# Block-sorted attention and a squared-ReLU FFN: the values of batches 1 to 3 sorted as rows in four array tiles, and turned by way of DRAM

## The chip, the cores and the metric

The kernel runs on one core of a Trainium2 chip. The metric is the device time of one execution in microseconds (us), and the median over several runs is compared. The engines are named as the profile names them: PE is TensorE (PEld its weight loads), DVE is VectorE, ACT is ScalarE, POOL is GpSimd and SP is SyncE. Here SP only issues DMAs. All DMA queues share 16 DMA engines.

## The reference

Four batches, eight heads, 768 tokens in eight blocks of 96, 64 values per head. A small 8 x 8 matrix per head is turned into a soft permutation P by five rounds of exponential and row and column normalisation. Keys and values are mixed over blocks with P. Each query block attends to its sorted block. The result, as 3072 rows of 512, goes through a two-layer network.

```python
P = sort_net
for _ in range(5):
    P = P - np.max(P, axis=-1, keepdims=True)
    P = np.exp(P)
    P = P / (np.sum(P, axis=-1, keepdims=True) + 1e-09)
    P = P / (np.sum(P, axis=-2, keepdims=True) + 1e-09)
...
k_sorted = np.einsum('bhij,bhjcd->bhicd', P, k_b).reshape(B, H, S, D)
v_sorted = np.einsum('bhij,bhjcd->bhicd', P, v_b).reshape(B, H, S, D)
...
scores = scale * np.matmul(q_b, k_sb.transpose(0, 1, 2, 4, 3))
scores = scores - np.max(scores, axis=-1, keepdims=True)
attn = np.exp(scores)
attn = attn / (np.sum(attn, axis=-1, keepdims=True) + 1e-09)
return np.matmul(attn, v_sb).reshape(B, H, S, D).astype(np.float32)
...
h = x @ w_in
r = np.maximum(h, 0.0)
g = s * (r * r) + b
return (g @ w_out).astype(np.float32)
```

## The kernel before, in words

**Layout.** A batch is cut into two halves of 384 tokens (TG), so the network has eight token groups t = 2b + half. ffn1(t) makes the squared hidden layer of one group (L395): eight pairs of 128-wide columns, each pair 8 matmuls on PE (L408), a relu on ACT (L422) and a multiply on DVE (L423). ffn2(t) multiplies it with w_out (L427): three output tiles of 128 tokens with 16 matmuls each (L433), then DVE scales and adds a bias (L454) and SP stores the tile (L457).

**Attention of one batch.** Raw keys, values and queries come by POOL's DMA queue, which casts to bf16 on the way (load, L84; load_q, L94, in eight DMAs of short rows). k_piece (L247) sorts 16 of 48 key positions with 32 matmuls of 64 columns, whose moving operand is a block-diagonal form of P (PD, build_pd L231); v_piece (L298) does the same for 16 of 64 value columns. For v_piece the raw values must lie with the value column outside and the position inside, so they are first copied into VP (permute, L165), by ACT for batch 0 and by POOL for the others (v_sort, L504, eight copies per batch). The sorted values stand in VS (L107), key position on the partitions and 66 numbers per head and block: 64 values and two ones. The ones make the sum of the attention weights come out of the same matmul as the attention output. s_piece (L311) makes the scores of one head pair and half, and their exponential on ACT; p_piece (L338) multiplies them with VS and DVE normalises into x; t_dma (L386) transposes x by a DMA of SP into XT, the input of ffn1. q_dma (L291) transposes the queries in the same way, in two DMAs.

**Order.** Each engine runs its instructions in the order of the program. The order is written by hand: ffn1 and ffn2 take a dictionary of slots, and the pieces in a slot are issued after the named pair of columns (ffn1) or group of four matmuls (ffn2, slots 0 to 11). Batch 0 is sorted at the start. While ffn2(2b) and ffn2(2b + 1) run, the pieces of batch n = b + 1 are woven in (L572 to L581). In ffn2(2b): K in slot 2, three of the four V pieces in slot 5, the last V and the first scores in slot 9, the first P in slot 11. The loads of batch 1 follow the weights on POOL's queue (L514); those of batches 2 and 3 are issued in the first slot of ffn1 (gated_loads, L555).

**Buffers.** rawp has two buffers each for raw keys, values and queries, psa three two-bank PSUM buffers that all pieces and ffn1 share, VP, KS and VS two each (for even and odd batches).

Of the kernel before, what the change touches and what calls it, by code (L numbers as in the profile page):

```python
# [9 lines left out]
FP = mybir.dt.float32  # L10
# [12 lines left out]
def kernel(  # L23
# [26 lines left out]
    KR = GAP + C2  # L50
    NG = NHP * NB
    VW = D + 2
    CK = 16
    scale = float(D) ** -0.5


    raw = [t.rearrange("b h (j z c) d -> b (h j z) (c d)", j=NB, z=2) for t in (q, k, v)]

    const = ctx.enter_context(tc.tile_pool(name="const", bufs=1))
    rawp = ctx.enter_context(tc.tile_pool(name="rawp", bufs=2))  # L60
    trp = ctx.enter_context(tc.tile_pool(name="trp", bufs=2))
    atp = ctx.enter_context(tc.tile_pool(name="atp", bufs=6))
    xp = ctx.enter_context(tc.tile_pool(name="xp", bufs=2))
# [3 lines left out]
    osb = ctx.enter_context(tc.tile_pool(name="osb", bufs=3))  # L67
    psa = ctx.enter_context(tc.tile_pool(name="psa", bufs=3, space=bass.MemoryType.PSUM))
    psb = ctx.enter_context(tc.tile_pool(name="psb", bufs=2, space=bass.MemoryType.PSUM))
    ctx.enter_context(tc.manual_schedule())  # L70


# [11 lines left out]
    def load(t, b, parts=1):  # L84
# [3 lines left out]
        for c in range(0, C2, n):  # L88
            nc.gpsimd.dma_start(out=ti[:, c:c + n, :].rearrange("p c d -> p (c d)"),
                                in_=raw["qkv".index(t)][b][:, c * D:(c + n) * D])  # L90

    QTOK = {}

    def load_q(b, ns=range(NB)):  # L94
# [4 lines left out]
        for n in ns:  # L99
# [2 lines left out]
    zeros = const.tile([128, 512], BF)  # L102
    nc.vector.memset(zeros[:, 0:128], 0.0)  # L103
    nc.vector.memset(zeros[:, 128:512], 0.0)  # L104
    VP = [const.tile([128, D, GAP], BF, name=f"vp{i}") for i in range(2)]
    KS = [const.tile([128, NG, 2, GAP], BF, name=f"ks{i}") for i in range(2)]
    VS = [const.tile([KR, 2 * NG, VW], BF, name=f"vs{i}") for i in range(2)]  # L107
    nc.vector.memset(VP[0][:, :, C2:GAP], 0.0)
    nc.vector.memset(KS[0][:, :, :, C2:GAP], 0.0)
    nc.vector.memset(sne[:, NB, :], 1e-9)  # L110

# [3 lines left out]
    idv = ident.rearrange("p (a e j z) -> p a e j z", a=NHP, e=2, j=NB)  # L115
    emat = const.tile([BH, B, 128], FP)
    nc.gpsimd.memset(emat, 0.0)
    nc.gpsimd.affine_select(out=emat, in_=emat, pattern=[[-H, B], [-1, H], [0, 2 * NB]], base=0,
                            channel_multiplier=1, compare_op=ALU.not_equal, fill=1.0)
    load("k", 0, 3)  # L120
    load_q(0, range(HB))
# [24 lines left out]
            fs = slice(c * (NF // 4), (c + 1) * (NF // 4))  # L146
            nc.gpsimd.dma_start(out=wo[:, fs, :], in_=wov[:, fs, :])

    def fill_vs(i):
        nc.gpsimd.memset(VS[i][:, :, D:VW], 1.0)  # L150
        nc.gpsimd.memset(VS[i][32:GAP, :, D:VW], 0.0)
        nc.gpsimd.memset(VS[i][32:C2, :, D:VW], 1.0)

    fill_vs(0)
    Z = []

    def warm(n, w=512):
# [4 lines left out]
                             start=True, stop=True)  # L162


    def permute(eng, b, src, cs=slice(0, C2), ds=slice(0, D)):  # L165
        o = VP[b % 2][:, ds, cs]
        i = src[:, cs, ds].rearrange("p c d -> p d c")
        if eng is nc.scalar:
            eng.copy(out=o, in_=i)
        else:  # L170
            eng.tensor_copy(out=o, in_=i)  # L171


    rstat = const.tile([BH, NB], FP)
    rrec = const.tile([BH, NB], FP)
    jsel = const.tile([128, NB], FP)
    bm = const.tile([128, 2 * 2 * NHP], FP)
    idle = [
        lambda: nc.vector.tensor_reduce(
            out=jsel, in_=ident.rearrange("p (h j z) -> p j h z", h=H, j=NB), axis=AX.XY, op=ALU.add),  # L180
# [8 lines left out]
    for it in range(5):  # L189
        nc.scalar.activation(out=sn, in_=sn, func=AF.Exp)  # L190
        if it >= 1:
            permute(nc.scalar, 0, v0f, slice((it - 1) * CV, it * CV))
        if it in (1, 2):
            idle[it - 1]()
        nc.vector.tensor_reduce(out=rstat, in_=sn, axis=AX.X, op=ALU.add)
        nc.vector.reciprocal(out=rrec, in_=rstat)
        nc.vector.tensor_tensor(out=sn, in0=sn, in1=rrec.broadcast_to([BH, NB, NB]), op=ALU.mult)
        if it == 4:
            break
        nc.vector.tensor_reduce(out=rstat, in_=sne.rearrange("p i j -> p j i"),  # L200
                                axis=AX.X, op=ALU.add)
        nc.vector.reciprocal(out=rrec, in_=rstat)
        nc.vector.tensor_tensor(out=sn, in0=sn, in1=spread(rrec, [[0, NB], list(rrec.ap[1])]),
                                op=ALU.mult)
# [11 lines left out]
                             rhs=sn.rearrange("p i j -> p (i j)"), start=True, stop=True)  # L216
        return pe

    def take_p(b0, n, pe):

        bs = slice(b0, b0 + n)
        tmp = rtp.tile([128, n * NB, NB], FP, tag=f"tmp{n}", name="tmp")
        nc.vector.tensor_tensor(out=tmp, in0=pe.rearrange("p b i j -> p (b i) j"),
                                in1=spread(jsel, [[0, n * NB], list(jsel.ap[1])]), op=ALU.mult)
        nc.vector.tensor_reduce(out=PT[:, bs].rearrange("p b i -> p (b i)"), in_=tmp, axis=AX.X,
                                op=ALU.add)
        cs = rtp.tile([128, n], FP, tag=f"cs{n}", name="cs")
        nc.vector.tensor_reduce(out=cs, in_=PT[:, bs], axis=AX.X, op=ALU.add)
        nc.vector.reciprocal(out=RC[:, bs], in_=cs)

    def build_pd(b):  # L231
        pd = const.tile([128, 2, 2, NG], BF, name=f"pd{b}")
        nc.vector.scalar_tensor_tensor(
            out=pd.rearrange("p e z (a i) -> p (e z a) i", i=NB),
            in0=spread(bm, [list(bm.ap[1]), [0, NB]]), scalar=RC[:, b:b + 1],
            in1=spread(PT[:, b], [[0, 4 * NHP], list(PT.ap[2])]), op0=ALU.mult, op1=ALU.mult)
        PD[b] = pd

    def evac(eng, out, in_):
        if eng == "A":  # L240
# [50 lines left out]
    def q_dma(b):  # L291
        qt = q_tile(b)
        for n0 in (0, HB):
            nc.sync.dma_start_transpose(
                out=qt[:, n0:n0 + HB].rearrange("p n a t -> p (n a) t"),
                in_=QTOK[b][:, n0:n0 + HB].rearrange("p n h d -> p (n h d)"))

    def v_piece(b, d0, eng):  # L298
        ps = psa.tile([128, CK, 2 * NG], FP, tag="a", name="tv")
        for d in range(CK):  # L300
            for z in range(2):
                nc.tensor.matmul(out=ps[z * GAP:(z + 1) * GAP, d, :],  # L302
                                 lhsT=VP[b % 2][:, d0 + d, :], rhs=PD[b][:, :, z, :],
                                 start=True, stop=True)
        evac(eng, VS[b % 2][:, :, d0:d0 + CK], ps[0:KR].rearrange("p d g -> p g d"))

    AT = {}
    X = {}
# [32 lines left out]
    def p_piece(b, half, hp, later=False):  # L341
        g0 = hp * NB + half * HB
        atf = AT.pop((b, half, hp)).rearrange("p e t -> p (e t)")
        if hp == 0:
            X[b, half] = xp.tile([BLK, HB, d_model], BF, tag="x", name="x")
        x = X[b, half]
        pv = psa.tile([128, 2, 512], FP, tag="a", name="pv")
        for e in range(2):
            for n in range(HB):
                c0 = (e * HB + n) * BLK  # L350
                m = 128 if c0 + 128 <= 2 * TG else BLK
                nc.tensor.matmul(out=pv[0:m, e, n * VW:(n + 1) * VW],  # L352
                                 lhsT=atf[:, c0:c0 + m], rhs=VS[b % 2][:, e * NG + g0 + n, :],
                                 start=True, stop=True)

        def norm():
            pvv = pv[0:BLK, :, 0:HB * VW].rearrange("p e (n w) -> p e n w", w=VW)
            rec = rtp.tile([BLK, 2, HB], FP, tag="rec", name="rec")
            nc.vector.reciprocal(out=rec, in_=pvv[:, :, :, D])
            nc.vector.tensor_tensor(  # L360
                out=x[:, :, hp * 128:(hp + 1) * 128].rearrange("p n (e d) -> p e n d", e=2),
                in0=pvv[:, :, :, 0:D],
                in1=rec.unsqueeze(3).broadcast_to([BLK, 2, HB, D]), op=ALU.mult)

        if later:
            return norm
        norm()
# [89 lines left out]
        nc.sync.dma_start(out=out[r0:r0 + 128, ns], in_=ot[:, ns])  # L457


    take_p(0, 1, spread_p(0, 1))  # L460
    build_pd(0)

    nc.gpsimd.tensor_copy(out=ones[:, 0:1], in_=PD[0][:, 0, 0, 0:1])
# [31 lines left out]
    nc.gpsimd.memset(sel, 0.0)  # L495
    for r in range(0, 128, 32):
        nc.gpsimd.memset(sel[r:r + 1], 1.0)
    nc.gpsimd.memset(VP[1][:, :, C2:GAP], 0.0)
    nc.gpsimd.memset(KS[1][:, :, :, C2:GAP], 0.0)
    fill_vs(1)  # L500
    for t, src in ((s_bc, moe_s), (b_bc, moe_b)):
        nc.gpsimd.dma_start(out=t, in_=src.to_broadcast([128, 1]))

    def v_sort(b):  # L504
        for i in range(8):
            permute(nc.gpsimd, b, RAW["v", b], ds=slice(i * 8, (i + 1) * 8))

    def loads(b):
        load("k", b)
        load("v", b)  # L510
        load_q(b)
        v_sort(b)

    loads(1)  # L514

# [19 lines left out]
        nc.scalar.activation(out=bias, in_=bps, func=AF.Copy, scale=b_bc)  # L535

    def K(b, i, eng): return lambda: k_piece(b, i * CK, eng)
    def V(b, i, eng): return lambda: v_piece(b, i * CK, eng)
    def SC(b, h, i): return lambda: s_piece(b, h, i)
    def SB(b, h, i): return lambda: s_banks(b, h, i)  # L540
    def P(b, h, i): return lambda: p_piece(b, h, i)
# [3 lines left out]
    def QB(b, n0, eng): return lambda: q_blocks(b, n0, eng)  # L545
# [2 lines left out]
    ffn1(0, {-1: [TP(0, 0, 2, "AD")], ("pre", 1): [QB(0, HB, "D"), QB(0, HB + 2, "D")],  # L548
             2: [SB(0, 1, 0)], 3: [SB(0, 1, 1), P(0, 1, 0)], 4: [SB(0, 1, 2), P(0, 1, 1)],
             5: [SB(0, 1, 3), P(0, 1, 2)], 6: [TP(0, 1, 0, "D"), P(0, 1, 3)]}, ahead=3)  # L550
    ffn1(1, {-2: [TP(0, 1, 2, "D")], 1: [lambda: take_p(1, B - 1, PB), PDB(1)], 4: [PDB(2)],
             5: [PDB(3), sum_w], 7: [make_bias]}, ahead=3)
    gate = const.tile([128, 1], BF)

# [7 lines left out]
    for b in range(B):  # L562
# [4 lines left out]
        if n == B:  # L567
            ffn2(2 * b, {})
            ffn2(2 * b + 1, {})
            break  # L570
        q_dma(n)
        s0 = {  # L572
            2: [K(n, 0, "A"), K(n, 1, "D"), K(n, 2, "A")],
            5: [V(n, 0, "D"), V(n, 1, "A"), V(n, 2, "D")],
            9: [V(n, 3, "D"), SC(n, 0, 0), SC(n, 0, 1)],
            11: [P(n, 0, 0), SC(n, 0, 2), SC(n, 0, 3)]}
        ffn2(2 * b, s0)
        ffn2(2 * b + 1, {0: [P(n, 0, 1)], 1: [P(n, 0, 2)],
                         2: [P(n, 0, 3), TD(n, 0), SC(n, 1, 0), SC(n, 1, 1)],
                         4: [P(n, 1, 0)], 5: [P(n, 1, 1), SC(n, 1, 2), SC(n, 1, 3)],  # L580
                         7: [P(n, 1, 2)], 8: [P(n, 1, 3), TD(n, 1)]})  # L581


# [28 lines left out]
```

## Time and profile before

| | us |
|---|---|
| Median of three runs (lowest, highest) | 229.03 (228.82, 230.14) |
| The profiled execution | 228.41 |
| Its span in the profile | 226.6 |
| PE busy in the span | 218.9 (97%) |
| DVE, ACT, POOL busy | 124.5, 99.5, 68.2 |
| ffn1 matmuls (L408), busy | 85.7 |
| ffn2 matmuls (L433), busy | 85.7 |
| V sorting matmuls (L302), busy | 10.0 |
| POOL's copies of values (L171), busy | 19.0 |

The profile shows one execution. Busy time of an engine is the time in which at least one instruction of it runs. The chain that ended last goes back from the last instruction, at each step to what released it, or to the instruction before it on its engine; a piece of work in it has a start and a duration. A group of instructions has its mean duration in ns, and ahead of it the engine's idle time with what ended it. Matmuls overlap in the pipeline, so the mean of one is longer than the distance between two.

### The profile page before, as it was taken

To read this page: it belongs to the slowest core of one execution; us is meant where nothing else is said; L and a number is where in the kernel's file an instruction comes from. 1 tells how busy PE (TensorE), PEld (TensorE's weight loads), DVE (VectorE), ACT (ScalarE), POOL (GpSimd) and SP (SyncE) were. 2 spreads that over 40 slices of the span, in tenths; PEclk is the share of its full clock that TensorE was granted. 3 is DMA by queue.
4 is the path that set the end of the run, shared out by engine and by line. 5 is a ranking of instruction groups with operands and counts; after the bars stand their busy time and mean duration, and the time that the engine had idled before them with its cause. 6 is when DMAs were issued, how large, how long until landed. Compare 5 with 4: busy or idle time off the path is not lost.

```text
span 226.6 us, 5806 instructions
## 1 busy us (share of the span) xinstructions
PE 218.9 (97%) x2542; PEld 133.2 (59%) x2542; DVE 124.5 (55%) x223; ACT 99.5 (44%) x128; POOL 68.2 (30%) x112
## 2 busy tenths in 40 slices
PE   7996999999999999999999999999999999999993
PEld 8985656655555556665555556655566566654452
DVE  6766467553647634498656634498557543441121
ACT  4966476564325225637143236627152246550000
POOL 8467797338400009291000028490000000000000
PEclk9999999999999999999999999999999999999999
DMA  5999999999711558993112459991123240001212
GB/s 190 238 105 133 181 164 206 207 196 136 164 49 49 129 151 136 188 166 72 49 47 73 138 120 176 176 171 36 49 95 67 100 114 0 4 0 46 94 49 93
DMA packets 53930, 25.82 MB, mean 114 GB/s; under 512 B 44944, under 2 KB 49296, under 8 KB 53904
## 3 DMA queue, kind: packets, MB, share of 16 engines
q0 software_dynamic: 30864, 12.85, 47.1%
q1 hardware_dynamic: 23040, 12.59, 20.9%
q8 instruction: 20, 0.33, 0.6%
q14 instruction: 6, 0.05, 0.1%
HBM read 27.27 MB, written 6.29 MB: 148 GB/s over the span
## 4 chain that ended last, share of the span: by engine, by line
PE 86%; DVE 5%; DMA 3%; POOL 2%; ACT 1%; issue 1%; POOLq 0%
PE ops L433 36%; PE hps L408 36%; PE pv L352 3%; PE tv L302 3%; DMA qtok<-in_q_dram 3%; PE sc L317 2%; PE tp L252 2%; PE ops L446 2%; POOL wi L131 1%; DMA sne<-in_sort_net_dram 1%; ACT rt L422 1%; POOL qtok L100 1%; ACT sne L190 1%; PE scb L332 1%; DVE rstat L200 0%
## 5 line engine op out<-in xcount | busy, mean ns | idle before, releaser
L408 PE MATMUL hps<-xt,wi 128*128 128x384 bf16 x512 | 85.7, 326 | 0.3 <-DMA qtok<-in_q_dram 0.3
L433 PE MATMUL ops<-wo,gt 128*128 128x512 bf16 x368 | 85.7, 379 | 0.0
L422 ACT ACTIVATE rt<-hps 128x768 bf16<-128x768 f32 x64 | 51.1, 811 | 53.4 <-PE hps L408 45.6
L423 DVE TENSOR_TENSOR gt<-rt 128x768 bf16<-128x768 bf16 x64 | 46.9, 739 | 41.2 <-ACT rt L422 40.4
L408 PEld LDWEIGHTS <-wi 128*128 128x128 bf16 x512 | 49.3, 98 | 33.5 <-issue 0.6
L433 PEld LDWEIGHTS <-gt 128*128 128x128 bf16 x368 | 33.7, 98 | 36.9 <-issue 0.6
L454 DVE SCALAR_TENSOR_TENSOR ot<-ops,s_bc,bias 128x512 f32<-128x512 f32 (+1 forms) x25 | 18.2, 730 | 30.8 <-PE ops L433 28.2
L322 ACT ACTIVATE at<-sc 112x768 bf16<-112x768 f32 x28 | 21.3, 808 | 30.3 <-PE sc L317 30.3
L100 POOL DMA_DIRECT2D qtok<-in_q_dram x32 | 24.9, 793 | 18.4 <-DMA rawv<-in_v_dram 9.0
L360 DVE TENSOR_TENSOR x<-pv,rec 96x512 bf16<-96x512 f32 x32 | 22.0, 687 | 1.1
L243 DVE CAST vs<-tv 112x1024 bf16<-112x1024 f32 x11 | 13.2, 1222 | 10.8 <-PE tv L302 10.7
L171 POOL COPY vp<-rawv 128x384 bf16<-128x384 bf16 x24 | 19.0, 849 | 0.0
L558 POOL COPY gate<-gt 128x1 bf16<-128x1 bf16 x2 | 0.4, 193 | 56.6 <-DVE gt L423 56.6
L352 PEld LDWEIGHTS <-at 112*128 112x128 bf16 (+1 forms) x256 | 12.8, 101 | 7.2 <-ACT at L322 1.1
L352 PE MATMUL pv<-vs,at 112*128 112x66 bf16 (+1 forms) x256 | 13.9, 195 | 1.0 <-DVE vs L243 1.0
L161 PE MATMUL z<-zeros 128*128 128x140 bf16 (+1 forms) x132 | 11.7, 256 | 1.2 <-DVE zeros L104 1.2
L302 PEld LDWEIGHTS <-vp 128*64 128x64 bf16 x512 | 9.0, 113 | 3.9 <-issue 3.6
L161 PEld LDWEIGHTS <-zeros 128*128 128x128 bf16 x132 | 10.1, 111 | 1.4 <-DVE zeros L103 1.0
L302 PE MATMUL tv<-pd,vp 128*64 128x64 bf16 x512 | 10.0, 197 | 0.9 <-issue 0.8
L241 ACT CAST ks<-tp 128x1024 bf16<-128x1024 f32 x8 | 8.1, 1012 | 4.0 <-PE tp L252 3.9
L131 POOL DMA_DIRECT2D wi<-in_moe_w_in_dram x16 | 8.6, 552 | 2.6 <-DMA wi<-in_moe_w_in_dram 0.9
L241 ACT CAST vs<-tv 112x1024 bf16<-112x1024 f32 x5 | 5.1, 1019 | 9.3 <-PE tv L302 9.3
(76 smaller groups left out, 104.3 us busy)
## 6 DMA issues: line engine op xcount, KB each, us to landing
out_dram<-ot SPq DMA_DIRECT2D x23, 256.0 KB, 2.0
qtok<-in_q_dram POOLq DMA_DIRECT2D x32, 96.0 KB, 9.5
rawk<-in_k_dram POOLq DMA_DIRECT2D x3, 768.0 KB, 6.8
rawv<-in_v_dram POOLq DMA_DIRECT2D x3, 768.0 KB, 10.0
wi<-in_moe_w_in_dram POOLq DMA_DIRECT2D x16, 128.0 KB, 5.2
wo<-in_moe_w_out_dram POOLq DMA_DIRECT2D x4, 512.0 KB, 10.8
v0f<-in_v_dram SPq DMA_DIRECT2D x4, 384.0 KB, 4.3
rawk<-in_k_dram POOLq DMA_DIRECT2D x3, 256.0 KB, 7.9
```

The costliest lines, as they stand in the source:

```text
L100: nc.gpsimd.dma_start(out=QTOK[b][:, n], in_=qv[:, n])
L161: nc.tensor.matmul(out=Z[0][:, 0:w], lhsT=zeros[:, 0:128], rhs=zeros[:, 0:w], start=True, stop=True)
L171: eng.tensor_copy(out=o, in_=i)
L302: nc.tensor.matmul(out=ps[z * GAP:(z + 1) * GAP, d, :], lhsT=VP[b % 2][:, d0 + d, :], rhs=PD[b][:, :, z, :], start=True, stop=True)
L322: nc.scalar.activation(out=at, in_=sc[0:KR, :, 0:TG], func=AF.Exp, scale=scale)
L352: nc.tensor.matmul(out=pv[0:m, e, n * VW:(n + 1) * VW], lhsT=atf[:, c0:c0 + m], rhs=VS[b % 2][:, e * NG + g0 + n, :], start=True, stop=True)
L360: nc.vector.tensor_tensor(out=x[:, :, hp * 128:(hp + 1) * 128].rearrange("p n (e d) -> p e n d", e=2), in0=pvv[:, :, :, 0:D], in1=rec.unsq ...
L408: nc.tensor.matmul(out=H1[i][:, f, 0:TG], lhsT=wi[:, hp, fc:fc + 128], rhs=xt[:, :, hp, :], start=(hp == 0), stop=(hp == NHP - 1))
L422: nc.scalar.activation(out=rt, in_=h, func=AF.Relu)
L423: nc.vector.tensor_tensor(out=gt[:, 2 * i:2 * i + 2, :], in0=rt, in1=rt, op=ALU.mult)
L433: nc.tensor.matmul(out=ops, lhsT=gt[:, f, m * 128:(m + 1) * 128], rhs=wo[:, f, :], start=(f == 0), stop=(f == NF - 1))
L454: nc.vector.scalar_tensor_tensor(out=ot[:, ns], in0=ops, scalar=s_bc, in1=BIAS[0][:, ns], op0=ALU.mult, op1=ALU.add)
```

## The change

Batch 0 is sorted as before. For batches 1 to 3 a new v_rows takes the place of v_piece. The raw values are loaded so that each half z of a block's positions has its own 64 partitions (load_z; the keys too). P, in block-diagonal form, becomes the weight (PV, 64 x 64) and the raw values are the moving operand, 512 columns at a time; two halves z of the rows and two parities y of the position give four matmuls in the four 64 x 64 quarters of the array. What comes out has head and block on the partitions and position and value along the row. It is evacuated into VO in rows of 96 numbers (VR), of which 32 were set to one at the start. SP writes them to a DRAM tile DV, six DMAs of 1024 rows of 192 bytes. v_back then reads DV into VS[1] with two DMAs of POOL, 48 partitions each, in rows of 12,288 bytes.

With this go: no copies on POOL (v_sort and VP[1] leave); one VS and one raw buffer for batches 1 to 3 (rawp has bufs=1); two more mask tiles and a PV per batch, built on DVE; the rows of emat ordered for z outside; two larger memsets on POOL before the loads of batch 1 (VS[1][32:64] and VO); values loaded ahead of keys; V in slot 0, K in slot 3, scores in slots 10 and 11, and the P pieces in pairs from slot 3 of ffn2(2b + 1) on; for batch 1, q_dma is issued after the writes of DV.

```diff
+    VR = 96
...
+    rawz = [t.rearrange("b h (j z c) d -> b z (h j) (c d)", j=NB, z=2) for t in (q, k, v)]
...
-    rawp = ctx.enter_context(tc.tile_pool(name="rawp", bufs=2))
+    rawp = ctx.enter_context(tc.tile_pool(name="rawp", bufs=1))
...
+    def load_z(t, b):
+        ti = rawp.tile([128, C2, D], BF, tag=f"raw{t}", name=f"raw{t}")
+        RAW[t, b] = ti
+        for z in range(2):
+            nc.gpsimd.dma_start(out=ti[z * 64:(z + 1) * 64].rearrange("p c d -> p (c d)"),
+                                in_=rawz["qkv".index(t)][b, z])
...
+    VS = [const.tile([KR, 2 * NG, w], BF, name=f"vs{w}") for w in (VW, VR)]
+
+    DV = drp.tile([BLK, 2 * NG, VR], BF, name="dv")
+    VO = const.tile([128, 2, C2 // 2, VR], BF)
...
+    for z in range(2):
+        em = emat[:, 1:B, z * 64:(z + 1) * 64]
+        nc.gpsimd.affine_select(out=em, in_=em, pattern=[[-H, B - 1], [-1, H], [0, NB]], base=-H,
+                                channel_multiplier=1, compare_op=ALU.not_equal, fill=1.0)
...
+        PD[b] = build(b, bmz if b else bm, "pd").rearrange("p (e z a) i -> p e z (a i)", e=2, z=2)
+        if b:
+            PV[b] = build(b, bmv, "pv").rearrange("p m i -> p (m i)")
...
+    def v_rows(b, i, eng):
+
+        src, n = RAW["v", b], 8
+        ps = psa.tile([128, 2, n, D], FP, tag="a", name="vo")
+        for y in range(2):
+            for z in range(2):
+                zs, ys = slice(z * 64, (z + 1) * 64), slice(y * 64, (y + 1) * 64)
+                c0 = i * 2 * n + y
+                nc.tensor.matmul(out=ps[ys, z], lhsT=PV[b][zs], rhs=src[zs, c0:c0 + 2 * n - 1:2, :],
+                                 start=True, stop=True, tile_position=(z * 64, y * 64))
+        vo = VO[:, :, i * n:(i + 1) * n, :]
+        evac(eng, vo[:, :, :, 0:D], ps)
+        dv = DV.rearrange("(z t c y) g w -> z t (y g) c w", z=2, y=2, c=n)
+        for z in range(2):
+            nc.sync.dma_start(out=dv[z, i], in_=vo[:, z])
+
+    def v_back(b):
+
+        for z in range(2):
+            nc.gpsimd.dma_start(out=VS[1][z * GAP:z * GAP + C2].rearrange("k g w -> k (g w)"),
+                                in_=DV[z * C2:(z + 1) * C2].rearrange("k g w -> k (g w)"))
...
-    nc.gpsimd.memset(VP[1][:, :, C2:GAP], 0.0)
     nc.gpsimd.memset(KS[1][:, :, :, C2:GAP], 0.0)
-    fill_vs(1)
+    nc.gpsimd.memset(VS[1][32:GAP], 0.0)
+    nc.gpsimd.memset(VO, 1.0)
...
     def loads(b):
-        load("k", b)
-        load("v", b)
+        load_z("v", b)
+        load_z("k", b)
         load_q(b)
-        v_sort(b)
...
-    ffn1(1, {-2: [TP(0, 1, 2, "D")], 1: [lambda: take_p(1, B - 1, PB), PDB(1)], 4: [PDB(2)],
+    ffn1(1, {-2: [TP(0, 1, 2, "D")], 1: [masks_z, lambda: take_p(1, B - 1, PB, jselz), PDB(1)], 4: [PDB(2)],
              5: [PDB(3), sum_w], 7: [make_bias]}, ahead=3)
...
-        q_dma(n)
+        if b:
+            q_dma(n)
         s0 = {
-            2: [K(n, 0, "A"), K(n, 1, "D"), K(n, 2, "A")],
-            5: [V(n, 0, "D"), V(n, 1, "A"), V(n, 2, "D")],
-            9: [V(n, 3, "D"), SC(n, 0, 0), SC(n, 0, 1)],
-            11: [P(n, 0, 0), SC(n, 0, 2), SC(n, 0, 3)]}
+            0: [V(n, 0, "D"), V(n, 1, "A"), V(n, 2, "D"), lambda: v_back(n)]
+               + ([] if b else [lambda: q_dma(n)]),
+            3: [K(n, 0, "A"), K(n, 1, "D"), K(n, 2, "A")],
+            10: [SC(n, 0, 0), SC(n, 0, 1)],
+            11: [SC(n, 0, 2), SC(n, 0, 3)]}
         ffn2(2 * b, s0)
-        ffn2(2 * b + 1, {0: [P(n, 0, 1)], 1: [P(n, 0, 2)],
-                         2: [P(n, 0, 3), TD(n, 0), SC(n, 1, 0), SC(n, 1, 1)],
-                         4: [P(n, 1, 0)], 5: [P(n, 1, 1), SC(n, 1, 2), SC(n, 1, 3)],
-                         7: [P(n, 1, 2)], 8: [P(n, 1, 3), TD(n, 1)]})
+        ffn2(2 * b + 1, {3: [P(n, 0, 0), P(n, 0, 1)],
+                         5: [P(n, 0, 2), P(n, 0, 3), TD(n, 0)],
+                         6: [SC(n, 1, 0), SC(n, 1, 1)], 7: [SC(n, 1, 2), SC(n, 1, 3)],
+                         8: [P(n, 1, 0), P(n, 1, 1)],
+                         10: [P(n, 1, 2), P(n, 1, 3), TD(n, 1)]})
```

## The prediction

> **What bounds the kernel now.** I read the page's first part, then the chain that ended last, the chain cut to one stage, POOL's timeline and the DMA view of short windows.
>
> ```profile
> PE 218.9 (97%) x2542; PEld 133.2 (59%) x2542; DVE 124.5 (55%) x223; ACT 99.5 (44%) x128; POOL 68.2 (30%) x112
> ...
> PE 86%; DVE 5%; DMA 3%; POOL 2%; ACT 1%; issue 1%; POOLq 0%
> ```
>
> TensorE is busy for 218.9 of 226.6 us and carries 86% of the chain. From 24 us to the end it never waits 0.5 us at once. So a matmul taken away shortens the kernel, work moved between the other engines does nothing, and a transfer counts only if TensorE comes to wait for it. The stage at stake is ffn2 of t = 2, into which batch 2 is woven (the chain, from 102 us):
>
> ```profile
> 102.30 2.59 PE ops L433 x12
> 104.89 1.64 PE tp L252 x96
> 106.53 2.70 PE ops L433 x12
> 109.23 1.64 PE tv L302 x96
> 110.86 3.56 PE ops L433 x16
> 114.42 0.63 PE tv L302 x32
> 115.05 0.45 PE sc L317 x16
> 115.49 1.83 PE ops L433 x8
> 117.33 0.27 PE pv L352 x8
> ```
>
> The reader sees start and duration: four ffn2 matmuls (one slot) take 2.59 / 3 = 0.86 us, K sorting 1.64, V sorting 1.64 + 0.63 = 2.27, two score pieces 0.45, one p_piece 0.27; a burst makes the next group about 0.1 longer (2.70 against 2.59). Two gaps elsewhere matter to the new path. POOL's timeline:
>
> ```profile
> 32.84 0.96 POOL L499 MEMSET ks<- 128x1024 bf16 x1
> ...
> 35.60 0.57 POOL L89 DMA_DIRECT2D rawk<-in_k_dram  x1
> 36.13 0.58 POOL L89 DMA_DIRECT2D rawv<-in_v_dram  x1
> ...
> 96.42 6.29 POOL L171 COPY vp<-rawv 128x384 bf16<-128x384 bf16 x8
> ```
>
> A POOL memset costs 0.93 ns per element and partition; the loads of batch 1 are issued from 35.6 us; the sorting copies run after the loads. And the DMA view from 97 to 104 us, where short rows move on both queues:
>
> ```profile
> GB/s 152 243 146 138 145 148 153 145 155 155 151 151 158 156 167 215 233 191 123 112 173 293 288 290 288 186 16 0 0 31 167 165 174 190 221 219 219 215 238 253
> DMA packets 6392, 1.20 MB, mean 172 GB/s; under 512 B 6391, under 2 KB 6391, under 8 KB 6391
> ...
> q0 software_dynamic: 3392, 0.42, 96.3%
> q1 hardware_dynamic: 2999, 0.76, 58.3%
> ```
>
> Slices of 0.175 us. Query rows alone (0.42 MB / 3392 = 124 B) run at some 152 GB/s, or 1220 packets per us; query transposes alone (253 B) at 290 GB/s, 1140 per us. No short row is written to DRAM here, and that is the change's unknown.
>
> [...] The trace agrees for two: K's 64-column matmuls come every 1.64 / 96 = 17 ns, less than 64 columns at 0.86 us / 2048 columns (27 ns). Four at once, no run shows yet.[...]
>
> **The change part by part.** Call T0 the start of ffn2(2b).
>
> *V matmuls.* 128 of 64 columns per batch (2.27 us) become 12 of 512 columns in four tiles. One streams for 0.86 / 4 = 0.215 us; four together, three rounds, 0.65 us[...]. Saved 1.5 us, for three batches 4.5. Bounds: no overlap, 12 x 0.215 = 2.6, a loss of 0.3 each; pairs only, 1.3, a gain of 1.0. I take four, since pairs are seen[...].
>
> *Removed and added beside TensorE.* POOL loses 19.0 us of sorting copies (24 x 849 ns), which slowed DVE's gt multiplies beside them (DVE's timeline from 96.7 us: six in 9.35 us, against 0.56 each). TensorE was not held by either, so zero, but it frees DVE for the evacuations. masks_z and three pv builds are some 0.9 us of DVE in slot 1 of ffn1(1) (rows of 0.27 and 0.35), hidden by three rt buffers and a new pair only every 1.3 us. The two later affine selects fall into POOL's 4.8 us of waiting for the first pd. Zero for both; uncovered they would cost under 1 us once.
>
> *The new path.* PE ends V piece 0 at T0 + 1.1; DVE finishes the last gt at about T0 + 1.5 (relu 0.81, multiply 0.56), evacuates piece 0 until 2.75 and piece 2 until 4.0 (1.22 each), ACT piece 1 until 2.6 (1.02). SP issues six writes from T0 + 2.75. A store lands 2.0 us after issue, of which 0.65 is its data (256 KB at 390 GB/s), so the fixed part is 1.35 and data flow from T0 + 4.1. Writes: 6144 rows of 192 B. Low, at the 1140 per us of the transposes, 5.4 us[...]. I take 6.5, above the low end since no record shows such writes at their best.
>
> Read back: two POOL DMAs, 1.18 MB in 12 KB rows. Key and value loads land 6.8 and 10.0 us after issue (the page's DMA part) and are issued 0.56 apart, so they land 3.8 apart: 1.57 MB of source, 0.79 MB written, take 3.8, and the fixed part is 3.0. 1.18 MB take 2.9 at the rate of the source side and 5.7 at that of the written side: 6 to 9 in all. I take 6.3, nearer the source side, since nothing is cast. VS is there at T0 + 4.1 + 6.5 + 6.3 = T0 + 16.9.
>
> Needed: the first P sits behind 16 slots (13.8), V 0.75, K 1.64, four score pieces 0.9, restarts 0.4: T0 + 17.5. So batches 2 and 3 fit by 0.6 us; I put 0.15 of stall on each for what the stores add. Point of no stall: 7.1 us of write data; each further us is one us of stall per batch. Queued behind a waiting P are all later matmuls, DVE's norms, the transpose of x and so the next ffn1; nothing else on PE can go ahead.
>
> *P later.* The first four P move to slots 3 and 5. The last norm ends about 1.8 us after its P, the transpose lands 3.8 later: 5.7. Up to ffn1 lie 6 slots, four score pieces and four P, 5.2 + 0.9 + 1.1 = 7.2. Zero, with 1.5 to spare.
>
> *Batch 1.* POOL's VP memset (0.96) and fill_vs (0.7) go; VS[1][32:64] has 6144 elements per partition and VO 4608, at 0.93 ns together 10.0 us. The loads start about 8 us later, near 43.5. DMA was working off wo until about 43 (POOL's last wait on wo ends at 44.07), so data resume near 45 and the loads end 2 us later: V at 50, before its use at 53.1; K at 53, before 56.5; queries from 56 to 58, instead of 54 to 56. SP issues the query transposes behind the six writes, and their data queue behind them. Writes start near 56.2, share with the queries for 2 us, end near 62.5; the first transpose lands 3 us later, 65.6. The first scores at slot 10 want it at 52.3 + 9.5 + 0.75 + 1.64 + 0.2 = 64.4. Stall 1.2 us (0 if writes are fast, 7 if they take twice as long). VS then lands near 70.6; P, pushed to 71.0, does not wait again. Stores behind SP's transposes have three ot buffers.
>
> Sum: 4.5 - 1.2 - 0.3 = 3.0 us off. The profiled execution took 228.41 us (span 226.6), so 225.4; the median 229.03 lies 0.6 above it, and so 226.0.
>
> **Rivals.** *Short DRAM writes cost double* (slower). Place: P at slot 3, and batch 1's scores. Writes take 10.8 us: VS at T0 + 21.2, a stall of 3.7 for batches 2 and 3; in batch 1 writes end near 68.5, the transpose lands at 71.3, a stall of 6.9. Stalls 14.3, saving 4.5: 9.8 slower, 238.8. It decides from about 8.1 us of write data (1.0 more stall in each stage eats the rest). For it:[...] no such write is in the trace. Against it: short SBUF writes run at over 1100 per us.
>
> *Tiles overlap only in pairs, or not at all.* V takes 1.3 or 2.6 us: 3.0 saved or 1.0 lost, then the stalls: 227.5 or 231.5. For it: K's pairs reach 17 ns and not 13.5.[...]
>
> *The start-up stage alone eats it.* Batch 1's loads come later than I think, or the transposes queue longer: a stall of 4.2 there, and 229.0. For it: that stage has all queues busy. Against: nothing of it repeats at T0 = 102.3 and 152.3, where loads end before.
>
> **How the numbers follow.** Forecast 0.48; double write cost 0.32; pairs or none 0.08 (half faster, half slower); start-up 0.12 (0.08 same, 0.04 slower). This measurement can tell about 1% from no change. Faster 0.48 + 0.04 = 0.52; same 0.08; slower 0.32 + 0.04 + 0.04 = 0.40. The forecast's own range is 223.8 (no stall, V at 0.65, fewer restarts) to 227.5 (half a us more in each stage). To leave out two in ten, the whole one goes from 223.8 to 237.5, most of the way into the double cost.
>
> **What would show it.** Right: V's matmuls in three bursts of about 0.22 us; busy TensorE near 214.5; a wait of one to two us at the first scores of batch 1 on the query transposes, and none over 0.5 at the P pieces. Wrong: a wait of P for VS in all three stages, writes that land more than 9 us after the first issue, or V's chain piece above 1.3 us.

## The result, and the profile after

The changed kernel takes 248.94 us (246.97 to 250.14 in four runs) against 229.38: ratio 1.084, interval 1.076 to 1.092. The forecast had 226.0 and faster. The profiled execution took 249.09 us, with a span of 247.3. In all that follows, executions that took over 1.5% more than the fastest of the same kernel are left out of medians and ratios.

The page, parts 1, 2 and 4 (busy time; the granted clock by slice; the chain by engine and by line):

```profile
PE 223.3 (90%) x2194; PEld 129.1 (52%) x2194; DVE 109.9 (44%) x226; ACT 99.6 (40%) x128; POOL 63.8 (26%) x100
...
PEclk9999999999959799999999799999999799999999
...
PE 71%; DMA 19%; DVE 3%; issue 2%; ACT 1%; SPq 1%; POOL 0%; POOLq 0%
```

Before, DMA held 3% of the chain and now it holds 19%. PE's busy time rose although its matmuls became fewer, and the clock row, all 9 before, has a hole in each of the three stages. The waits of the matmuls say where:

```profile
PE pv L407 <- DMA vs<-dv: 12.9, 3, 4.7
...
PE sc L372 <- DMA qt<-qtok: 4.3, 1, 4.3
```

(Total us, times, longest.) The P pieces wait for VS in all three stages, and the first scores of batch 1 for the query transposes. The chain in the stage of batch 2, with the V matmuls of batch 3 at its end:

```profile
116.94 0.38 SPq L345
...
119.66 5.76 DMA dv<-VO
...
126.11 0.39 POOL vs L350
...
127.02 8.92 DMA vs<-dv
...
136.07 0.97 PE pv L407 x16
137.05 3.09 PE ops L488 x8
...
168.78 0.86 PE ops L488 x4
169.65 0.77 PE vo L339 x12
170.42 2.70 PE ops L488 x12
```

This stage's ffn2 began at T0 = 114.2. The first write is issued at T0 + 2.7 (116.94). The write in the chain is the fifth of the six, issued at 119.66. With it the first half (z = 0) of the sorted values is in DRAM, at T0 + 11.2 (125.43), and POOL issues the first read at T0 + 11.9. The sixth write is issued at 120.75 and ends the second half; the DMA view of 122 to 122.9 us has its time to landing:

```profile
dv<-VO SPq DMA_DIRECT2D x1, 192.0 KB, 5.7
```

So all six have landed at T0 + 12.2. The second read is issued at T0 + 12.8 (127.02) and lands 8.92 us later, at T0 + 21.7. TensorE is ready for the P piece at T0 + 17.7 and stands for 4.19 us. Eight ffn2 matmuls after the wait then take 3.09 us, where eight took 1.83 in the kernel before. The new V matmuls, twelve in 0.77 us, are as fast as was hoped.

The stages, from the start of ffn2(2b) to the start of the next ffn1 (from PE's timeline), in us:

| Kernel | batch 1 | batch 2 | batch 3 |
|---|---|---|---|
| before | 29.2 | 29.2 | 29.2 |
| after | 41.4 | 33.6 | 33.5 |
| after, transit left out (no_trip, below) | 27.6 | 27.6 | 27.6 |

The stages make +20.9 of the +20.7 us in span. Of these, -4.7 is the saving (3 x 1.57, by the last row), +17.2 are the four waits (4.29, 4.66, 4.19, 4.06), and the remaining +8.4 has to be something that comes with the waits.

### The profile page after: what moved, and what is told of

Its sections match the earlier page's. It is cut to its first block, busy times and chain, and to the rows that moved or that the text cites. A ratio compares the mean times of both kernels' runs of the same rounds, so it can differ in the third digit from the quotient of the medians.

```text
span 247.3 us, 5157 instructions
## 1 busy us (share of the span) xinstructions
PE 223.3 (90%) x2194; PEld 129.1 (52%) x2194; DVE 109.9 (44%) x226; ACT 99.6 (40%) x128; POOL 63.8 (26%) x100
## 4 chain that ended last, share of the span: by engine, by line
PE 71%; DMA 19%; DVE 3%; issue 2%; ACT 1%; SPq 1%; POOL 0%; POOLq 0%
PE hps L463 33%; PE ops L488 22%; DMA vs<-dv 13%; DMA dv<-VO 6%; PE z L176 5%; PE pv L407 4%; PE ops L501 1%; PE tp L285 1%; PE sc L372 1%; PE tv L357 1%; ACT rt L477 1%; SPq L345 1%; DVE gt L478 1%; PE vo L339 1%; DVE vs L276 0%
## 5 line engine op out<-in xcount | busy, mean ns | idle before, releaser
L488 PE MATMUL ops<-wo,gt 128*128 128x512 bf16 x368 | 91.7, 400 | 0.0
L463 PEld LDWEIGHTS <-wi 128*128 128x128 bf16 x512 | 49.3, 98 | 33.5 <-issue 0.8
L488 PEld LDWEIGHTS <-gt 128*128 128x128 bf16 x368 | 35.4, 103 | 43.0 <-issue 8.3
L478 DVE TENSOR_TENSOR gt<-rt 128x768 bf16<-128x768 bf16 x64 | 35.6, 559 | 45.3 <-ACT rt L477 45.1
L407 PE MATMUL pv<-vs,at 112*128 112x66 bf16 (+1 forms) x256 | 12.4, 201 | 13.9 <-DMA vs<-dv 12.9
L407 PEld LDWEIGHTS <-at 112*128 112x128 bf16 (+1 forms) x256 | 11.4, 106 | 18.4 <-issue 15.0
L350 POOL DMA_DIRECT2D vs<-dv x6 | 3.2, 532 | 45.7 <-DMA dv<-VO 44.5
L414 DVE RECIPROCAL rec<-pv 96x8 f32<-96x8 f32 x32 | 6.3, 198 | 18.1 <-PE pv L407 18.1
L372 PE MATMUL sc<-qt,ks 64*128 64x96 bf16 x224 | 8.1, 214 | 4.4 <-DMA qt<-qtok 4.3
L176 PEld LDWEIGHTS <-zeros 128*128 128x128 bf16 x132 | 10.8, 116 | 1.4 <-DVE zeros L114 1.0
L372 PEld LDWEIGHTS <-ks 64*128 64x128 bf16 x224 | 5.7, 99 | 10.3 <-issue 8.6
L276 DVE CAST VO<-vo 128x1024 bf16<-128x1024 f32 x6 | 7.1, 1218 | 0.7 <-PE vo L339 0.7
```

Of the source, the lines that this page charges most:

```text
L176: nc.tensor.matmul(out=Z[0][:, 0:w], lhsT=zeros[:, 0:128], rhs=zeros[:, 0:w], start=True, stop=True)
L372: nc.tensor.matmul(out=sc[:, e, n * BLK:(n + 1) * BLK], lhsT=KS[b % 2][pr, g0 + n].rearrange("p z c -> p (z c)"), rhs=QT[b][pr, half * HB ...
L407: nc.tensor.matmul(out=pv[0:m, e, n * VW:(n + 1) * VW], lhsT=atf[:, c0:c0 + m], rhs=VS[min(b, 1)][:, e * NG + g0 + n, 0:VW], start=True, s ...
L463: nc.tensor.matmul(out=H1[i][:, f, 0:TG], lhsT=wi[:, hp, fc:fc + 128], rhs=xt[:, :, hp, :], start=(hp == 0), stop=(hp == NHP - 1))
L478: nc.vector.tensor_tensor(out=gt[:, 2 * i:2 * i + 2, :], in0=rt, in1=rt, op=ALU.mult)
L488: nc.tensor.matmul(out=ops, lhsT=gt[:, f, m * 128:(m + 1) * 128], rhs=wo[:, f, :], start=(f == 0), stop=(f == NF - 1))
```

## The experiments

Where a ratio is given it is to the kernel before on the same chip; the changed kernel itself has 1.084.

**What the matmuls save, and what the transit costs.** no_trip leaves out both directions, no_back only the reads (VS stays at ones).

```diff
-            0: [V(n, 0, "D"), V(n, 1, "A"), V(n, 2, "D"), lambda: v_back(n)]
+            0: [V(n, 0, "D"), V(n, 1, "A"), V(n, 2, "D")]
```

(no_trip also drops the loop with nc.sync.dma_start in v_rows.)

> Both the writes to DRAM and the read back are left out; the sorting matmuls and their evacuation stay, and VS is ones for batches 1 to 3. Theory: nothing waits, the saving of the matmuls shows by itself: 229.4 - 4.5 = about 225. Rival (the matmuls in array tiles or the new order of the pieces cost something themselves): 228 or more.

> The read back of the sorted values into VS is left out, so batches 1 to 3 use a VS of ones; the writes to DRAM stay. Theory (the wait of P for the read back costs most): the three P stalls of 4.7, 4.2 and 4.1 us and the cold clock after them go, the wait of batch 1's first scores on the query transposes stays with its cold clock: 4.5 us of matmuls saved, 4.3 + 1.5 lost, so 229.4 + 1.3, about 231. Rival (the slow short writes themselves disturb the other transfers): still above 238.

Measured: no_trip 223.81 us, 0.977 (0.972 to 0.983); no_back 231.46, 1.011 (1.006 to 1.016). Without the transit the change is worth 5 us, as the theory had it. With the writes alone the stages of batches 2 and 3 take 27.6 us each and that of batch 1 33.2, so the writes hurt nobody but batch 1's query transposes, and the reads make the rest.

**The cold clock.** In the 4.1 us after the wait of batch 2 the clock granted to TensorE was 0.59 of full speed in the mean (the last but two of these numbers; the windows view of the changed kernel):

```profile
136.07:140.20 4.13, 4.13 (x32) 2.15 (x33) 1.69 (x4) 0.00 (x0) 0.00 (x0) 0.59 0.03 11
```

To see what that costs, twenty matmuls on zeros (4.3 us) fill each of the four places where TensorE idled.

```diff
+        w = psa.tile([128, 2, 512], FP, tag="a", name="wz")
+        for _ in range(n):
+            nc.tensor.matmul(out=w[:, 0], lhsT=zeros[:, 0:128], rhs=zeros, start=True, stop=True)
...
-        ffn2(2 * b + 1, {3: [P(n, 0, 0), P(n, 0, 1)],
+        ffn2(2 * b + 1, {3: [lambda: fill(20), P(n, 0, 0), P(n, 0, 1)],
```

> 20 matmuls on zeros (4.3 us) are put ahead of the first P of each batch and ahead of the first scores of batch 1, where TensorE idled 4.1 to 4.7 us. Theory (after an idle time of over 4 us TensorE runs at half clock for some 3 us, which costs about 1.5 us at each of four places): the granted clock stays at 1.0 and the time falls from 249 to about 243. Rival (the waits alone make the loss): no change, 249.

Measured: 246.75, 1.080 (1.073 to 1.087). That interval overlaps the changed kernel's, so the whole time does not decide. The stages do: 38.1, 32.6 and 32.3, together 5.6 us shorter than 41.4, 33.6 and 33.5. Against 27.6 each they are longer by the inserted work (8.6, 4.3, 4.3) and what is left of the waits (1.57, 0.47, 0), within 0.4. The extra time at the lower clock is gone: it had been 4.8 us in the stage of batch 1, with two waits, and 1.8 in each of the others, which is the unexplained 8.4. Part of the gain is hidden because ffn2 began 1.8 us later in this profiled run (53.8 against 52.0), which varies between runs of kernels with the same start.

**The rows of the writes.** The same bytes go to DRAM in rows of 1536 B, which puts values in a wrong order.

```diff
-        dv = DV.rearrange("(z t c y) g w -> z t (y g) c w", z=2, y=2, c=n)
+        dv = DV.rearrange("k g w -> (k g w)").rearrange("(z t p w) -> z t p w", z=2, t=3, p=128)
         for z in range(2):
-            nc.sync.dma_start(out=dv[z, i], in_=vo[:, z])
+            nc.sync.dma_start(out=dv[z, i], in_=vo[:, z].rearrange("p c w -> p (c w)"))
```

> The same bytes of VO go to the same DRAM tile in rows of 1536 B instead of 192 B, which puts the values in a wrong order. Theory of the forecast's rival (short rows to DRAM are what is slow): 3.0 us of write data at 390 GB/s instead of 7.4, so the writes land some 3 us sooner (5.5 instead of 8.5 after the first issue), the P stall falls from 4.1 to about 1, and the total to about 238. Rival (SP's issue of six DMAs and the read back set the time, not the rows): the writes land less than 1.5 us sooner, total above 244.

Measured: 233.20, 1.023 (1.014 to 1.032). SP's timeline, after and then long_rows (start, duration, number of DMAs):

```profile
116.94 6.01 SPq L345 DMA_DIRECT2D dv<-VO  x6
```

```profile
111.51 2.77 SPq L345 DMA_DIRECT2D dv<-VO  x6
```

Short rows also hold SP: 6.0 us for six issues against 2.8, and 9.0 in the stage of batch 1, where the query loads run beside them. With long rows the last write lands 3.3 us sooner after T0 (8.9 against 12.2) and the first half 4.2 us sooner (7.0 against 11.2), so the first read is issued 4.2 us sooner (T0 + 7.7 against 11.9). VS lands at T0 + 17.9, and the waits of batches 2 and 3 shrink to 0.31 and 0.82 us. Batch 1's scores wait 1.32 instead of 4.29, though its P still waits 4.25. So the short rows cost about 4 us of transit per batch; what part of it is SP's issue and what part the data, this run doesn't separate. The rate of the short rows stands in the DMA view of the changed kernel from 117 to 127 us, in slices of 0.25 us:

```profile
GB/s 0 0 0 91 189 181 192 182 181 184 194 182 175 158 207 182 181 235 188 182 163 182 180 187 135 19 185 187 187 212 330 362 299 52 316 369 328 41 25 25
```

They move at some 180 GB/s, which is 940 rows of 192 B per us, from about 117.9 to 124.4 us (the faster slices after that are output stores). That is about four fifths of the 1140 packets per us of the query transposes, not half.

**The read back.** Half of each row only:

```diff
-            nc.gpsimd.dma_start(out=VS[1][z * GAP:z * GAP + C2].rearrange("k g w -> k (g w)"),
-                                in_=DV[z * C2:(z + 1) * C2].rearrange("k g w -> k (g w)"))
+            nc.gpsimd.dma_start(
+                out=VS[1][z * GAP:z * GAP + C2, 0:NG].rearrange("k g w -> k (g w)"),
+                in_=DV[z * C2:(z + 1) * C2, 0:NG].rearrange("k g w -> k (g w)"))
```

> Only half of each row is read back (6 KB of 12 KB for each of 48 + 48 partitions), the other half of VS stays at ones. Theory (the time of the read back goes with the bytes, some 130 GB/s): from the first issue to the last landing about 6 us instead of 9.8, the P stall of batches 2 and 3 falls from 4.1 to about 0.5, total about 238. Rival (a fixed latency, queueing or hand-over makes the 10 us): landing still above 8 us, total above 245.

Measured: 231.44, 1.011 (1.008 to 1.014). From the first issue to the last landing 5.2 and 5.6 us in batches 2 and 3 instead of 9.8, and no wait of P for VS: their stages take 27.4. (Batch 1's scores still wait 5.66 us for the query transposes.) So most of the time goes with what is read: 0.59 MB more take 4.2 to 4.6 us, some 130 to 140 GB/s. The rows are halved with the bytes, so this run alone does not tell the two apart. The page's DMA issues for the whole kernel, after (KB each, us to landing):

```profile
dv<-VO SPq DMA_DIRECT2D x18, 192.0 KB, 4.9
vs<-dv POOLq DMA_DIRECT2D x6, 576.0 KB, 7.9
```

Six more runs ask what makes it slow. The stores beside it:

```diff
-        nc.sync.dma_start(out=out[r0:r0 + 128, ns], in_=ot[:, ns])
+        if t not in (0, 2, 4):
+            nc.sync.dma_start(out=out[r0:r0 + 128, ns], in_=ot[:, ns])
```

> The output stores of token groups 0, 2 and 4, which run beside the writes and the read back, are left out (their rows of the output aren't written). Theory (the read back, 1.18 MB in 8.9 us after its last issue, shares the DMA engines with two stores of 256 KB): the landing falls from 9.8 us to about 7, the P stall of batches 2 and 3 from 4.1 to about 1.5 with no cold clock, and 249 becomes about 240. Rival (the read back is slow by itself): landing 9 us or more, no change.

Measured: 251.07, 1.096 (1.089 to 1.104), landing 10.3 us after the first issue in batch 2. Beside this read 0.26 MB of stores move instead of 0.61, and it lands no sooner, so the stores are not the cause. Next, one DMA over all of VS (DV gets the gap's rows of zeros), and the issue by SP:

```diff
-        for z in range(2):
-            nc.gpsimd.dma_start(out=VS[1][z * GAP:z * GAP + C2].rearrange("k g w -> k (g w)"),
-                                in_=DV[z * C2:(z + 1) * C2].rearrange("k g w -> k (g w)"))
+        nc.gpsimd.dma_start(out=VS[1].rearrange("k g w -> k (g w)"),
+                            in_=DV[0:KR].rearrange("k g w -> k (g w)"))
```

> DV gets 16 rows of zeros between the halves, and one DMA reads 112 rows of 12 KB into all of VS, in place of two DMAs of 48. Theory[...]: the landing after the first issue falls from 9.8 us to about 6.5 in batches 2 and 3, the P stall from 4.1 to about 1, no cold clock there: about 240. Rival (the reads are slow because the stores run beside them, or because of a fixed latency): 9 us and more, 247 to 250.

> The two reads of 48 rows are issued by SP instead of POOL, in SP's order behind the six writes. Theory A (48 partitions are what makes the reads slow): from the first issue to the last landing still 8 us or more, P stall 3.5 or more, total about 247. Theory B (POOL's descriptors make them slow): 6 us or less, P stall of batches 2 and 3 under 1, total about 238. Batch 1's scores wait in any case, and longer, if the transposes now stand behind the reads on SP.

> One read of 112 rows, as in the run with one read, but issued by SP. With theory A the number of partitions reached is what counts and this is no better than POOL's single read (8 us from issue to landing, stalls of 3 to 4). With theory B, or if both count, 1.38 MB at the 400 GB/s of the start-up loads of SP take 3.4 us, landing 5.5 us after issue, and batches 2 and 3 do not stall: total about 237.

And, on SP, four pieces of 3 KB per row, or 128 rows:

> The single read of 112 rows by SP is cut into four DMAs of 112 rows of 3 KB, the row length at which the start-up load of values moved near 400 GB/s. Theory (12 KB rows[...] are what is slow): landing about 6 us after the first issue instead of 8.8, no P stall, 240 or less. Rival (the row length doesn't matter): 8 us or more, 250 as with one read by SP.

> The single read by SP takes 128 rows (16 more of zeros)[...]. Theory (the uneven spread of 112 or 48 rows over engines and partitions is what is slow): 1.57 MB at 400 GB/s land 6 us after issue, in spite of the added bytes, P stall under 1, 240 or less. Rival (bytes alone): 9.5 us, 252.

Landing after the first issue in batches 2 and 3, and the bytes over that time:

| Read back | MB | us | GB/s | Total us, ratio |
|---|---|---|---|---|
| POOL, 2 x 48 rows (after) | 1.18 | 9.8, 9.8 | 120 | 248.94, 1.084 |
| SP, 2 x 48 rows (two_sp) | 1.18 | 10.2, 9.5 | 120 | 251.44, 1.100 |
| POOL, 112 rows (one_read) | 1.38 | 8.8, 7.9 | 165 | 248.21, 1.085 |
| SP, 112 rows (one_sp) | 1.38 | 8.8, 7.4 | 170 | 250.87, 1.099 |
| SP, 128 rows (rows128_sp) | 1.57 | 7.8, 7.4 | 206 | 247.65 (one execution) |
| SP, 112 rows in 3 KB pieces (pieces_sp) | 1.38 | 8.7, 7.0 | 176 | 248.99, 1.088 |

The queue does not matter: POOL and SP agree (9.8 and 9.8 us against 10.2 and 9.5). Nor does the length of the rows matter much: the last of the four pieces lands when one read by SP would. The third and the fourth piece in batch 2, issued at 133.29 and 133.76 us (DMA view of 133.4 to 133.7 and of 133.9 to 134.1 us), and P's waits for VS in the whole run:

```profile
vs<-dv SPq DMA_DIRECT2D x1, 336.0 KB, 5.3
vs<-dv SPq DMA_DIRECT2D x1, 336.0 KB, 7.3
PE pv L408 <- DMA vs<-dv: 1.0, 2, 0.5
```

P waits at most 0.5 us there because it starts at 138.66, when the third piece has landed (138.6), and not because the whole is there sooner (141.1): small DMAs let the first user go on with a part.

The spread over partitions does seem to matter: 128 rows land no later than 112 (7.8 and 7.4 us against 8.8 and 7.4), though they are 14% more bytes, and 112 in one DMA sooner than 96 in two. Part of the second difference is that two reads have two issues, 0.9 us apart, and that a fixed part weighs less on more bytes. No run changes the partitions alone, so this has the direction of theory A and does not prove it. Nor could it account for all: 206 GB/s into 128 partitions is still under the 370 to 440 GB/s that single slices show during the start-up loads of values in the kernel before (128 partitions, rows of 3 KB). What makes reads out of this DRAM tile slow stays open.

None of the five other ways to read made the kernel faster, though the reads became up to 2.8 us quicker. The four runs with 112 or 128 rows also write zeros to DV ahead of batch 1's loads, and batch 1's V matmuls wait 1.7 to 4.1 us for their values there, so these totals are not the price of the read alone. In batch 1 a read on SP stands ahead of the query transposes, and the scores wait 12 to 14 us. In batches 2 and 3 of pieces_sp the stores behind the reads hold DVE's ot buffers for 7.0 and 5.6 us, and P waits for DVE (2.09 and 0.87 us).

**Batch 1's loads.** VO is filled in POOL's early waiting time, VS[1] behind the loads.

```diff
+    nc.gpsimd.memset(VO, 1.0)
     Z = []
...
-    nc.gpsimd.memset(VS[1][32:GAP], 0.0)
-    nc.gpsimd.memset(VO, 1.0)
...
     loads(1)
+    nc.gpsimd.memset(VS[1][32:GAP], 0.0)
```

> POOL's two memsets no longer stand ahead of batch 1's loads: VO is filled in POOL's early waiting time, VS[1] after the loads. Theory (the forecast's step: the late loads make the query transposes late): the wait of batch 1's first scores falls from 4.3 us to about 2, total down by 2 to 4 us with the cold clock, about 245. Rival (the transposes are late because they queue behind the short-row writes on SP[...]): the wait stays above 3.5 us and the total within 1 us of 249.

Measured: 247.99, 1.084 (1.078 to 1.089); the scores wait 4.24 us, as before. The rival is right. SP's timeline in the changed kernel shows why:

```profile
54.73 8.97 SPq L345 DMA_DIRECT2D dv<-VO  x6
63.89 4.45 SPq L327 DMA_TRANSPOSE qt<-qtok  x2
```

The transposes are issued when the six writes have left SP, whenever the queries landed. long_rows agrees: there SP is done with the six in 3.0 us, and the wait is 1.32.

**Starting earlier.** v_early moves V of batches 2 and 3 into slots 3 to 5 of the ffn1 before; hybrid_early does the same and sorts batch 1 in the old way.

```diff
-            ffn1(2 * b + 1, {})
+            ffn1(2 * b + 1, {3: [V(n, 0, "D")], 4: [V(n, 1, "A")],
+                             5: [V(n, 2, "D"), lambda: v_back(n)]} if n < B else {})
```

> For batches 2 and 3 the V matmuls and the whole way through DRAM move into slots 3 to 5 of the ffn1 before (some 5 us earlier); batch 1 is unchanged. Theory (only the length of the chain write, semaphore, read back matters, 4.1 us too long): no P stall in batches 2 and 3, stages of 27.7 us instead of 33.6, so 249 - 12 = 237. Rival (beside the loads of queries the way gets longer by as much, or ffn1 loses its PSUM buffers to V): stages above 30, 242 or more.

> As the one before for batches 2 and 3, while batch 1 is sorted in the old way (POOL's copies, 64-column matmuls, old slots), with the two large memsets of POOL behind its loads. Theory (the stage of batch 1 loses 12 us to the late loads and to transposes queued behind the writes, the others nothing once they start early): 29.2 + 27.7 + 27.7 for the three stages, 3 us under the kernel before: about 226. Rival (moving V into ffn1 costs as much as it saves): 229.

Measured: 250.36, 1.097 (1.089 to 1.105) and 231.06, 1.010 (1.005 to 1.015). My theory failed for v_early. The reads were issued 8 us earlier relative to T0 and landed 16.6 us after the first issue (chain of v_early):

```profile
121.13 0.04 POOLq L350
121.17 0.52 issue
121.69 15.56 DMA vs<-dv
137.26 0.14 issue
137.39 1.09 PE pv L407 x16
```

They ran beside the query transposes that SP issued at 117.9; that these are the cause is likely but not shown, since no run takes them away from there. And V in ffn1 costs that pair 1.9 us for 0.8 us of matmuls. V and the hidden layer share psa, and 0.54 us of it is a wait of the hidden layer for DVE to empty a buffer of V. In hybrid_early the stages are 29.2, 28.2 and 26.8, but the two ffn1 pairs 22.7 instead of 20.8: the same sum as before. Its profiled ffn2 began 1.8 us later than in the kernel before (53.9 against 52.1), which makes up the rest.

**A version that hides the transit.** Batch 1 in the old way; V of batches 2 and 3 in slots 9 and 10 of the ffn2 of the stage before, P and scores in their old slots. In ahead the values of batch 3 are loaded behind the read back of batch 2; in ahead_order behind batch 2's keys and queries; in ahead_late, which the diff shows, the read back itself is issued behind those loads.

```diff
+    def ahead_v(m):
+        if m >= B:
+            return {}
+        return {9: [V(m, 0, "A")], 10: [V(m, 1, "A"), V(m, 2, "D")]}
...
     def loads(b):
-        load_z("v", b)
         load_z("k", b)
         load_q(b)
+        if b > 1:
+            v_back(b)
+        if b == 2:
+            load_z("v", 3)
```

> Batch 1 sorted in the old way; for batches 2 and 3 the V matmuls stand at the end of the ffn2 of the stage before (slots 9 and 10), so the way through DRAM has a whole ffn1 pair (some 20 us) more; their values are loaded a stage earlier; P and scores in the old slots. Theory (the matmul saving is real, 1.57 us per batch, and only the time of the transit spoilt it): stages of 29.2 + 0.8, 27.6 and 27 us, no wait of P, total 3 us under the kernel before, about 225.5. Rival (the DMA traffic slows the loads and stores of the other stages by as much): 228 or more.

> The run ahead, with the values of batch 3 loaded behind batch 2's keys and queries on POOL instead of ahead of them. Theory (its stage of batch 2 lost 2.2 us to keys that came late, and about 1 us to the cold clock after it): that wait goes, and the time falls from 227.5 to about 225, 1.5% under the kernel before. Rival (that wait was made by something else): no change, 227.5.

> As the run ahead_order, but POOL issues the read back of a batch behind the loads of its keys and queries instead of ahead of them, so that POOL no longer waits for the DRAM writes before it can issue loads. Theory (in the two runs before, loads held up behind the read back took 2.2 to 2.7 us of the 3 us saved): no wait of keys or queries, no wait of P (it is needed some 10 us after the read back lands), 225.5, 1.5% under the kernel before. Rival (the traffic of writes and reads makes something else wait): 227 or more.

Measured: 227.49, 0.994 (0.991 to 0.996); 227.45, 0.994 (0.992 to 0.997); 227.14, 0.991 (0.987 to 0.994). (The 22 executions of ahead_order spread widely, from 225.78 to 232.03; the median of all of them is 228.61, which is hardly a gain.) The first two moved the wait (2.23 us on batch 2's keys, then 2.69 on its query transposes, in profiled executions of 230.04 and 229.25 us) without a gain from one to the other. In ahead_late P never waits for VS, and what is left is

```profile
PE sc L377 <- DMA qt<-qtok: 1.3, 1, 1.3
```

It has the lowest median, some 2 us under the kernel before, though its interval overlaps those of the other two. The 225.5 that I expected of it was not reached.

## Why the prediction was wrong

*The matmuls.* Right: 0.77 us per batch where 0.75 had been taken (0.65 for three rounds, the rest an estimate), 1.57 saved for 1.5. The rival of overlap only in pairs is out. *The work beside TensorE* cost and gained nothing on the path, as said.

*The writes.* Mis-sized by 1.6 us: all six had landed at T0 + 12.2, where T0 + 4.1 + 6.5 gives 10.6. The rate was right. The short rows moved for about 6.5 us, as taken, and began some 0.4 us earlier than forecast. But the last landing came some 2 us after the last row (both estimated from the DMA view above), and the sum had its whole fixed part ahead of the data and nothing behind. The sign of being wrong came true: the sixth write landed 9.5 and 9.3 us after the first issue in batches 2 and 3, and 12.5 in batch 1. The rival that doubled the writes (10.8 us of data, twice the 5.4 at the rate of the transposes; the factor was assumed, no trace shows it) did not happen in that form. Its total, 238.8, and its mechanism of stalls at P and at batch 1's scores come closest to what was seen, and I gave it 0.32.

*The read back.* This is the step that failed most: 6.3 us were taken, between 6 and 9, and from the landing of the sixth write to VS it took 9.5 (0.6 until the second read is issued, 8.9 to land). In the forecast's own terms, fixed part and data, the first half landed 6.3 us after its issue and the second half 3.6 us after the first: some 7.1 us of data (165 GB/s) and 2.7 fixed, where 3.3 and 3.0 were taken. I had taken a rate near that of the source side of a 128-partition load for DMAs into 48 partitions; the written side of the same load, 5.7 us, would have been nearer. This is 3.2 of the 4.9 us by which VS came later than T0 + 16.9; the writes are the rest.

*The margin.* With VS at 16.9 and the need at 17.5 (measured 17.7), the forecast had 0.6 us of slack in a sum of four latencies, each known to a us or two only. Either error alone is more than that. long_rows and half_back show how near the edge it is: 4 us off either link, and the waits of batches 2 and 3 are gone or under 0.9 us.

*The cost of a wait.* Missing altogether: a wait of 4 us costs 1.8 us more in slow matmuls afterwards (warm_wait). In the changed kernel the clock granted in the 4.1 us after the waits of P (4.66, 4.19 and 4.06 us) was 0.59 in the mean each time, and 0.50 in the 4.0 us after that of batch 1's scores (4.29 us); eight matmuls after the wait of batch 2 took 3.09 us instead of 1.83. Some shorter waits had the same effect: 2.54 us in rows128_sp and 3.02 us in one_read (last section).

*Batch 1.* Predicted 1.2 us of stall, measured 4.29 at the scores and 4.66 at P, 4.8 of cold clock on top. The mechanism, transposes behind the writes on SP, was named, but SP's own time for short-row DMAs (9.0 us for six) was left out: the writes landed at 67.2 where the forecast had them end near 62.5, and the first transpose at 68.4 instead of 65.6. Left out too was what the other traffic does to the reads, the second of which landed 13.7 us after its issue there. The late loads were not a cause (memset_late). *P later* was right: no ffn1 waited for its transpose.

## What to carry to other kernels

The transit through DRAM was here a sum of issue, data, landing, hand-over, and data and landing again, 21.7 us from T0 in all. Place such a sum where the slack is larger than its whole uncertainty, here an ffn1 pair (20.8 us) instead of a few slots. Take a DMA's rate from one that is like it on the side that is written, in the number of partitions too (here 120 GB/s into twice 48 partitions and 206 into 128), and give the landing behind the last byte a term of its own (some 2 us for these writes, an estimate from the DMA view). And price a wait of TensorE at more than its length once the clock drops behind it (1.8 us more here for a wait of 4).

## What the runs showed of the hardware that I had not expected

Six DMAs of 1024 rows of 192 B keep SP's queue for 6.0 us, six of 128 rows of 1536 B for 2.8. 1.18 MB into twice 48 partitions came at 120 GB/s whichever queue issued it, 1.57 MB into 128 partitions at 206, and 1.38 MB in four DMAs of 3 KB rows landed hardly sooner than in one of 12 KB rows (8.7 and 7.0 us against 8.8 and 7.4). The same reads took 9.8 us in one place and 16.6 where query transposes ran beside them.

How long a wait has to be before the clock drops was not the same each time. By PE's timelines eight ffn2 matmuls take 1.89 us at the full clock, and four 1.04. In these runs slow matmuls followed every wait of TensorE of 3.2 us or more: after those of P, 3.22 us (two_sp) to 6.62 us (no_stores), the next eight took 2.85 to 3.55 us, and after those of batch 1's scores, 4.03 us (no_back) to 14.30 us (two_sp), the next four took 1.89. Of shorter waits of P, those of 2.54 us (rows128_sp, batch 2) and 3.02 us (one_read, batch 1) were followed by eight in 3.01 and 3.10 us too, while after those of 2.30 us (one_sp, batch 3) and 3.01 us (one_read, batch 3) eight took 1.89.
